# Second MLP, first layer: the first weight group as eight plain products instead of seven products of sums

## The chip, the cores and the metric

The kernel runs on one core of one Trainium2 chip. Times are device microseconds of one execution. The core's engines are TensorE (PE, with its weight loads PEld), VectorE (DVE), ScalarE (ACT), GpSimd (POOL) and SyncE (SP, which issues the DMAs). They run side by side and wait for one another by semaphores; each takes its own instructions in a fixed order.

## What is computed

Three stages follow one another: attention with a tanh cap on the scores, a gated MLP with RMS norm, and a second MLP. Only the last matters here.

```python
def _moe2_ref(x, w_in, w_out):          # x: 896 x 768, w_in: 768 x 2048
    h = x @ w_in
    g = h * (1.0 / (1.0 + np.exp(-h)))
    return (g @ w_out).astype(np.float32)
```

The change lies in the first 256 columns of `h = x @ w_in` and their silu.

## The kernel before, in words

Activations are kept transposed: features on the 128 partitions, 448 tokens (one of two batches) on the free axis. Products are made at nearly fp32 accuracy from two rounded halves of each operand: a high half (a rounded copy, mostly by ACT) and a low half (what the rounding left, a subtraction by DVE). A 128x128 block times 448 columns takes three matmuls: high times high, high times low, low times high; this text calls the three a triplet.

Every large matrix product is a 2x2 block product in Strassen-Winograd's form: seven block products of sums in place of eight plain ones. For the layer `h = x @ w_in`, `x` is cut into four operands, named by half of the features (K) and token batch: 11, 12, 21, 22. Each has three blocks of 128 features, `j` = 0 to 2. DVE turns them in place into T1 = 12 - 11, T3 = 22 - 12, T2 = 22 - T1 and T4 = 21 - T2 (`token_sums`, line 660), and each of 11, 21, 22, T1 to T4 is split into halves (`halves`: cast by ACT, low half by DVE on line 652).

The weights come in units of 128 hidden columns, two units `u`, `v` a group, eight groups i0 to i7. A unit is loaded by DMA and converted from its 8-byte form by two ACT operations (lines 349, 352) and one of DVE (line 355, tile `wz`). `sums` then makes four sums of `u` and `v` on DVE (lines 383, 386, 389, 392; tiles `zs`, `zq`), and `split` cuts `u`, `v` and the sums into halves (casts by ACT on line 287, low halves by DVE on line 370; tiles `wh`/`wl`, `sh`/`sl`, `qh`/`ql`).

`group` makes the seven products of a group, each of three triplets, on line 670: 11 and 21 with `u`, T2 with the sum, T1 with `v`, T3 with the sum, T4 with `v`, 22 with `zq`. They accumulate in PSUM banks of three rings, X (3 banks), Y (3) and Z (2). Partial results are read out between products by `keep` (ACT copies) and combined by three `add`s (DVE, line 773); silu follows on ACT (line 797).

The layer before it (the output layer of the gated MLP) writes the four operands from its own seven products, in the order 1, 2, 5, 6, 7, 3, 4. So 11 comes first (product 2), then 22 (product 7), then 12 (product 3, added from the Y banks on line 890), and 21 last (product 4, copied from the X banks by ACT).

The order of instructions is not that of the code. Each operation is entered with a list of engines and estimated costs, what it reads and writes, the buffers that it takes, and a priority from `turn` and a table by kind. A planner (`Plan.order`, eight rounds) lays out all operations after attention, sets each one's priority again from when its users are due, and keeps the best layout. GpSimd gets no work in this phase. A tile with one buffer of a name (`q5`, `p0`, ...) waits until all users of the one before are done.

Of the kernel before, what the change touches and what calls it, by code (L numbers as in the profile page):

```python
# [29 lines left out]
ROUNDS = 8  # L30
XS = 0.5
PE = 6
SWITCH = 0.1
WIN = dict(PE=0.05,ACT=0.50,DVE=0.50,Pool=0.25,SP=0.1,none=0.0)
BIAS1 = dict(ACT=0.0,DVE=0.0,Pool=0.0)
# [162 lines left out]
def fused_kernel(ctx: ExitStack, tc: tile.TileContext, qkv, cap, g, wg, wv, wo, wi2, wo2, out):  # L198
# [17 lines left out]
    S = NT // B  # L216
    P = 128
# [5 lines left out]
    KD = NP  # L223
# [4 lines left out]
    DH = DM // 2  # L228
# [4 lines left out]
    wp = ctx.enter_context(tc.tile_pool(name="wp", bufs=4))  # L233
# [3 lines left out]
    at = astack.enter_context(tc.tile_pool(name="at", bufs=2))  # L237
# [23 lines left out]
    op = plan.op  # L261
    tl = {}
# [11 lines left out]
    def half(name, n):  # L274
        return tl[name][:, n, :]
# [47 lines left out]
    def wide(name):  # L323

        t = tl[name]
        return t if len(t.shape) == 2 else f32(t.rearrange("p b s -> p (b s)"))[:, :UC]

    def convert(pl, u, turn, start=0.0, to="wz"):

        t = {}
        w, z, bufs = f"wraw_{u}", (f"wz_{u}.0", f"wz_{u}.1"), 1 if to[1:].isdigit() else 2

        def scale(e):
            words = wraw.pop(u)  # L340
            t["half"] = words.bitcast(U16).rearrange("p (n t) -> p n t", t=4)[:, :, 1]
            t["low"], high = (words.bitcast(U32).rearrange("p (n t) -> p n t", t=2)[:, :, i] for i in range(2))
            if bufs == 1:
                slot(f"wz_{u}", to)
            else:
                new(f"wz_{u}", wp, [P, UC], F32, to, bufs=2)
            z = wide(f"wz_{u}")
            t["zu"] = z.bitcast(U32)
            e.activation(out=z, in_=high.bitcast(F32), func=ACTF.Prelu, scale=2.0 ** -112, alpha=2.0 ** 32)  # L349

        def last(e):
            e.activation(out=t["low"], in_=t["half"], func=ACTF.Copy, scale=2.0 ** -13, bias=2.0 ** -14 - 0.5)  # L352

        def merge(e):
            e.scalar_tensor_tensor(t["zu"], t["zu"], 3, t["low"], ALU.logical_shift_left, ALU.bitwise_or)  # L355

        pl.op("wload", turn, lambda e: load_unit(u), {"SP": 0.45}, (), (w,), (("wraw", 2, w),), 0.66, 2.19, max(0.0, start - 6))
        pl.op("wscale", turn, scale, {"ACT": 0.81}, (w,), z, ((to, bufs, f"wz_{u}"),), start=start)
        pl.op("wshift", turn, last, {"ACT": 0.81}, z, (w,))
        pl.op("wlow", turn, merge, {"DVE": 0.87}, (w,), z)  # L360

    def split(pl, turn, z, reads, name, tags, pool, bufs=4, w=UC):

        h, l = f"h{name}", f"l{name}"

        def hi(e):
            copy(e, new(h, pool(), [P, w], F32R, tags[0], bufs=bufs), z())

        def lo(e):
            e.tensor_sub(new(l, pool(), [P, w], F32R, tags[1], bufs=bufs), z(), tl[h])  # L370

        full = w == UC
        pl.op("whi", turn, hi, {"ACT": 0.735, "DVE": 0.47} if full else {"ACT": 0.41, "DVE": 0.27}, reads, (h,), ((tags[0], bufs, h),))
        pl.op("wlo", turn, lo, {"Pool": 1.8, "DVE": 0.87} if full else {"Pool": 0.95, "DVE": 0.47}, (*reads, h), (l,), ((tags[1], bufs, l),))

    def sums(pl, u, v, turn, wait=()):

# [271 lines left out]
    def halves(pl, kinds, turn, name, tag, x):  # L649

        pl.op(kinds[0], turn, lambda e: copy(e, first(0, name, tag), x[1]()), {"ACT": 0.47, "DVE": 0.31}, (x[0],), (name + ".0",), ((tag, 1, name),))
        pl.op(kinds[1], turn, lambda e: e.tensor_sub(half(name, 1), x[1](), half(name, 0)), {"DVE": 0.54, "Pool": 1.1}, (x[0], name + ".0"), (name + ".1",))  # L652

    def token_sums(pl, kinds, turn, b, t, t2="22"):


        steps = (("11", "12", "11"), (t2, "22", "11"), ("12", "22", "12"), ("21", "21", t2))
        for i in (0, 2, 1, 3) if t2 == "22" else range(4):
            o, x, y = steps[i]
            pl.op(kinds[0], turn + 0.02 * max(0, i - 1), lambda e, o=o, x=x, y=y: e.tensor_sub(b[o][1](), b[x][1](), b[y][1]()), {"DVE": 0.54},  # L660
                  [b[m][0] for m in {x, y} - {o}], (b[o][0],), b[o][2] if len(b[o]) > 2 else ())
        for n, o in (("T2", t2), ("T1", "11"), ("T3", "12"), ("T4", "21")):
            halves(pl, kinds[1:], turn + 0.02 * "T2 T1 T3 T4".split().index(n), *t[n], b[o][:2])


    def passes(ps, w, c, x, start, stop, more=False):

        wh, wl = (tl[f"{n}{w}"][:, c:c + P] for n in "hl")
        for r, (a, y) in enumerate(((wh, x[0]), (wh, x[1]), (wl, x[0]))):
            nc.tensor.matmul(out=ps, lhsT=a, rhs=y, start=start and r == 0, stop=stop and r == 2, skip_group_check=more)  # L670
# [13 lines left out]
    for h in range(2):  # L684
        a, z = slice(h * R, (h + 1) * R), slice((1 - h) * R, (2 - h) * R)
# [19 lines left out]
    yo = ("11", "21", "T2", "T1", "T3", "T4", "22")  # L705
# [11 lines left out]
    order = plan.order(ROUNDS)  # L717
# [10 lines left out]
    class Rest(Plan):  # L728
        def op(self, kind, turn, fn, on, *args, **kw):

            super().op(kind, turn, fn, {e: c for e, c in on.items() if e != "Pool"}, *args, **kw)

    rest = Rest(TP2, DUE2, WIN2, BIAS2)
    op = rest.op

    def bank(name, tag):
        return new(name, mm, [P, 512], F32, tag, bufs=BANKS[tag])

    def take(name, tag):
        return (tag, BANKS.get(tag, 1), name)  # L740

    def group(n, u, v, turn, x, outs, stag):
# [44 lines left out]
        add(Y, 1, c12)  # L787
        return X

    def weights(u, v, turn):  # L790
        convert(rest, u, turn)
        convert(rest, v, turn)
        sums(rest, u, v, turn)

    def silu(turn, o, name, i=None, reads=(), alloc=()):
        src = i or o
        op("silu", turn, lambda e: e.activation(out=o(), in_=src(), func=ACTF.Silu), {"ACT": 0.5}, reads, (name,), alloc)
# [27 lines left out]
    def into(name, n, tag, on=True):  # L825

        def o():
            if on and name not in tl:
                slot(name, tag)
            return f32(half(name, n))  # L830
        return f"{name}.{n}", o
# [3 lines left out]
    for i in range(NG):  # L835
        h0, h1 = f"H_0_{i}", f"H_1_{i}"
        ta, tb, t0, t1 = ct[2 * i % 4], ct[(2 * i + 1) % 4], f"p{13 + i}" if i else "p20", f"q{12 + i}"
# [7 lines left out]
        X = group(f"g{i}", *g2, 2 * i, xop, outs, stags[0])  # L845
        for (name, o, _), t in ((outs[0], 0.3), (outs[3], 0.7), (outs[1], 0.9)):
            silu(2 * i + t, o, name)
        name, o = into(ca, 1, ta)
        silu(2 * i + 0.8, o, name, lambda X=X: tl[X][:, :S], (X,))
        houts = [(*into(h0, 0, t0), ((t0, 1, h0),)), (*into(h1, 0, t1), ()), None, (*into(h1, 1, t1), ((t1, 1, h1),))]  # L850
        X = group(f"v{i}", *v2, 2 * i + (1 if i else 0.05), xop, houts, stags[1])
        for n, c in ((0, f"{ca}.0"), (3, f"{cb}.1"), (1, f"{cb}.0")):
            name, o, _ = houts[n]
# [44 lines left out]
    t0, uo, MH, KH = 2 * NG, 2 * MF, MO // 2, MF // 2  # L898
# [11 lines left out]
    ty = dict(zip(yo, ("q12 q13 q14", "p16 p17 p18", "q9 q10 q11", "p9 p10 p11", "p20 p14 p15", "p0 p1 p2", "q15 q16 q17")))  # L910

    def ytag(y, j):
        return ty[y].split()[j]
# [4 lines left out]
    for i, n in enumerate(seq):  # L918
# [16 lines left out]
        for k in range(KH):  # L935
            h, c = hb(pb, k)
# [3 lines left out]
        for r in range(KH * MH):  # L940
            k, j = divmod(r, MH) if n != 4 else divmod(r, KH)[::-1]
            ps, w, x = f"{bank_of}_o{j}", f"o{n}_{j}", f"B{n}_{k}"

            def mul(e, k=k, ps=ps, w=w, x=x, fresh=fresh):
                if fresh and k == 0:
                    bank(ps, ps[0])
                passes(tl[ps][:, :S], w, k * P, (half(x, 0), half(x, 1)), fresh and k == 0, k == KH - 1, not fresh)

            op("mul", tn + 0.0476 * r, mul, {"PE": 0.595}, (f"h{w}", f"l{w}", *both(x)), (ps,), (take(ps, ps[0]),) if fresh and k == 0 else ())
        for j in range(MH):  # L950
            X, Y, Z, tj = f"X_o{j}", f"Y_o{j}", f"Z_o{j}", tn + 0.7
# [13 lines left out]
                evac("y", tj, X, yf(1, j, 1), y1 + ".1") if n == 4 else None  # L965
    for j in range(MH):
        ys = {y: (f"y{i}_{j}.{n}", yf(i, j, n)) for y, i, n in (("11", 0, 0), ("12", 0, 1), ("22", 1, 0), ("21", 1, 1))}
        for y in ("11", "22", "21"):
            halves(rest, ("tyh", "tyl"), t0 + 6, f"{y}_y{j}", ytag(y, j), ys[y])
        token_sums(rest, ("ty", "tyh", "tyl"), t0 + 6, ys, {n: (f"{n}_y{j}", ytag(n, j)) for n in yo[2:6]})  # L970


    ui, t0 = uo + 2 * MO, t0 + 6
    stile = "q5 q6 q7 q8 p3 p4 p5 q0 q1 q2 p12 p13 p19 p6 p7 p8".split()
    for i in range(MF2 // 2):
        u, v = ui + 2 * i, ui + 2 * i + 1
        weights(u, v, t0 + i)
        a, c = f"S_{2 * i}", f"S_{2 * i + 1}"
        qa, qc = stile[2 * i:2 * i + 2]
        outs = [(*into(a, 0, qa), ((qa, 1, a),)), (*into(a, 1, qa), ()), None, (*into(c, 1, qc), ((qc, 1, c),))]  # L980
        X = group(f"i{i}", u, v, t0 + i, lambda y, k: f"{y}_y{k}", outs, f"q{3 + i % 2}")
        for (name, o, _), t in ((outs[0], 0.3), (outs[3], 0.7), (outs[1], 0.9)):
            silu(t0 + i + t, o, name)
        name, o = into(c, 0, qc)
        silu(t0 + i + 0.8, o, name, lambda X=X: tl[X][:, :S], (X,))


    uw, t0 = ui + MF2, t0 + MF2 // 2
# [69 lines left out]
    for i, n in enumerate(seq):  # L1058
# [22 lines left out]
        for k in range(K2):  # L1081
            f, names, _ = sa(pa, k)
# [122 lines left out]
```

## Time and profile before

| | |
|---|---|
| median of 3 runs | 610.73 us (609.28 to 611.03) |
| the profiled execution | 611.11 us, span 609.0 us from first to last instruction |
| PE matmul busy | 591.4 us, 97% |
| PE weight loads busy | 498.8 us, 82% |
| DVE busy | 522.6 us, 86% |
| ACT busy | 456.0 us, 75% |
| mean granted TensorE clock | 0.988 of full speed |

Busy shares are averages over the whole span. A stretch with another limit than the rest has to be looked up in the sums by stretch, and what an engine waited for in its timeline and in the chain of waits.

### The profile page before, as it was taken

How to read it: one execution, taken by the hardware profiler on the slowest of the kernel's cores; microseconds unless marked ns; L12 is line 12 of the kernel's file. 1: busy time of each engine (PE TensorE's matmuls, PEld its weight loads, DVE VectorE, ACT ScalarE, POOL GpSimd, SP SyncE). 2: the span in 40 equal slices, each digit the busy share in tenths (PEclk: the TensorE clock that was granted, in tenths of full speed). 3: DMA queues.
4: the chain of work that ended last, by engine and by line, in shares of the span. 5: the costliest groups of instructions: out<-in, count | busy, mean ns of one | idle time of the engine just before them, and what ended most of it. 6: DMA issues, size and time to landing. Idle time of an engine off the chain costs nothing.

```text
span 609.0 us, 8752 instructions
## 1 busy us (share of the span) xinstructions
PE 591.4 (97%) x3170; PEld 498.8 (82%) x3170; DVE 522.6 (86%) x952; ACT 456.0 (75%) x807; POOL 52.6 (9%) x71
## 2 busy tenths in 40 slices
PE   7999999999899999999999999879999999999997
PEld 4555565557689999999999999669999999999997
DVE  4898999994998989868699999997878799999981
ACT  5998998882577776776796784866888889976642
POOL 1132429332000000000000000000000000000000
PEclk9999999999899999999999999969999999999999
DMA  6123212220025445343466001411534455440001
GB/s 259 52 106 97 111 54 73 92 97 0 2 103 163 150 142 169 104 156 107 153 206 208 2 0 50 159 53 52 180 132 156 156 166 195 159 155 1 34 31 66
DMA packets 15627, 66.23 MB, mean 109 GB/s; under 512 B 1888, under 2 KB 3680, under 8 KB 15584
## 3 DMA queue, kind: packets, MB, share of 16 engines
q1 hardware_dynamic: 15552, 65.67, 31.5%
q8 instruction: 25, 0.41, 0.3%
q14 instruction: 18, 0.15, 0.1%
q0 software_dynamic: 32, 0.00, 0.0%
HBM read 62.92 MB, written 2.75 MB: 108 GB/s over the span
## 4 chain that ended last, share of the span: by engine, by line
PE 64%; DVE 7%; ACT 2%; issue 1%; DMA 1%; DVEq 0%
PE X L670 29%; PE Y L670 15%; PE X L1037 7%; PE Z L670 7%; PE Y L1037 4%; DVE q L652 1%; PE Z L1037 1%; DVE p L660 1%; DVE p L355 1%; DMA wraw<-in_wo 1%; DVE wl L370 1%; ACT q L287 0%; DVE p L633 0%; DVE p L890 0%; DVE q L1090 0%
## 5 line engine op out<-in xcount | busy, mean ns | idle before, releaser
L670 PE MATMUL X<-q,sh 128*128 128x448 f32 x216 | 64.8, 379 | 6.0 <-DVE q L652 4.1
L352 ACT ACTIVATE wraw<-wraw 128x768 uint32<-128x768 uint16 x68 | 61.8, 908 | 0.0
L287 ACT COPY p<-X 128x448 f32<-128x448 f32 x48 | 25.6, 534 | 38.7 <-PE X L670 36.3
L670 PEld LDWEIGHTS X<-q,sh 128*128 128x128 f32 x216 | 42.0, 195 | 12.5 <-DVE q L652 5.7
L452 DVE TENSOR_SCALAR_CACHE_REDUCE p<-p,ncap 128x448 f32<-128x448 f32 x72 | 45.9, 674 | 6.9 <-ACT p L444 6.6
L670 PE MATMUL X<-q,wh 128*128 128x448 f32 x168 | 48.5, 368 | 1.5 <-DVE q L652 0.9
L370 DVE TENSOR_TENSOR wl<-wz,wh 128x768 fp32r<-128x768 f32 x47 | 44.8, 955 | 5.1 <-ACT wh L287 4.4
L287 ACT CAST wh<-wz 128x768 fp32r<-128x768 f32 x48 | 40.0, 836 | 11.0 <-DVE wz L386 4.7
L670 PE MATMUL X<-p,wh 128*128 128x448 f32 x168 | 48.1, 367 | 0.0
L355 DVE SCALAR_TENSOR_TENSOR wz<-wz,wraw 128x768 uint32<-128x768 uint32 x44 | 42.0, 956 | 5.2 <-ACT wraw L352 5.1
L287 DVE COPY pe<-pt 128x448 f32<-128x448 f32 x72 | 41.5, 618 | 5.6 <-PE pt L529 4.7
L287 ACT CAST q<-p 128x448 fp32r<-128x448 f32 (+1 forms) x51 | 27.3, 549 | 20.0 <-DVE p L931 6.0
L670 PE MATMUL X<-q,sl 128*128 128x448 f32 x108 | 40.6, 376 | 0.0
L349 ACT ACTIVATE wz<-wraw 128x768 f32<-128x768 f32 x44 | 39.9, 910 | 0.7 <-DVE wl L370 0.3
L444 ACT ACTIVATE p<-s,tscl 128x896 f32<-128x896 f32 x36 | 35.0, 1001 | 6.5 <-PE s L437 6.4
L670 PE MATMUL Z<-p,wh 128*128 128x448 f32 x132 | 38.9, 375 | 0.8 <-DVE p L652 0.8
L670 PEld LDWEIGHTS X<-q,wh 128*128 128x128 f32 x168 | 31.5, 188 | 5.3 <-DVE q L652 1.7
L437 PE MATMUL s<-x 64*128 64x448 f32 x144 | 33.2, 570 | 0.4 <-ACT p L444 0.3
L670 PEld LDWEIGHTS X<-p,wh 128*128 128x128 f32 x168 | 31.4, 188 | 2.6
L548 PE MATMUL av<-pe,x 128*64 128x448 f32 x144 | 31.7, 549 | 0.0
L287 ACT CAST p<-p 128x448 fp32r<-128x448 f32 (+1 forms) x47 | 25.3, 551 | 8.5 <-PE Y L1037 4.4
L670 PE MATMUL X<-q,wl 128*128 128x448 f32 x84 | 30.8, 367 | 0.3 <-DVE wl L370 0.3
(250 smaller groups left out, 1657.6 us busy)
## 6 DMA issues: line engine op xcount, KB each, us to landing
wraw<-in_wo SPq DMA_DIRECT2D x28, 768.0 KB, 4.3
wraw<-in_wi SPq DMA_DIRECT2D x16, 768.0 KB, 4.4
wraw<-in_wg SPq DMA_DIRECT2D x12, 768.0 KB, 4.6
wraw<-in_wv SPq DMA_DIRECT2D x12, 768.0 KB, 4.4
x<-in_qkv SPq DMA_DIRECT2D x11, 512.0 KB, 3.7
x<-in_qkv SPq DMA_DIRECT2D x14, 256.0 KB, 4.1
out<-q SPq DMA_DIRECT2D x12, 192.0 KB, 1.8
out<-zq SPq DMA_DIRECT2D x2, 192.0 KB, 1.9
```

The source lines that it names most:

```text
L287: e.tensor_copy(out=o, in_=i) if e is nc.vector else e.copy(out=o, in_=i)
L349: e.activation(out=z, in_=high.bitcast(F32), func=ACTF.Prelu, scale=2.0 ** -112, alpha=2.0 ** 32)
L352: e.activation(out=t["low"], in_=t["half"], func=ACTF.Copy, scale=2.0 ** -13, bias=2.0 ** -14 - 0.5)
L355: e.scalar_tensor_tensor(t["zu"], t["zu"], 3, t["low"], ALU.logical_shift_left, ALU.bitwise_or)
L370: e.tensor_sub(new(l, pool(), [P, w], F32R, tags[1], bufs=bufs), z(), tl[h])
L437: nc.tensor.matmul(out=ps[:, s, :S], lhsT=q_of(p, s, c), rhs=k_of(p, s), start=True, stop=True)
L444: nc.scalar.activation(out=o, in_=i, func=ACTF.Tanh, scale=tscl)
L452: nc.vector.tensor_scalar(t, t, ncap, None, ALU.mult, ALU.min, accum_out=tl[nb][:, n:n + 1])
L548: nc.tensor.matmul(out=tl[av][s * D:(s + 1) * D, :S], lhsT=v[:, (2 * k + s) * D:(2 * k + s + 1) * D], rhs=tl[f"pe_{p}_{m}"], start=k == 0, ...
L652: pl.op(kinds[1], turn, lambda e: e.tensor_sub(half(name, 1), x[1](), half(name, 0)), {"DVE": 0.54, "Pool": 1.1}, (x[0], name + ".0"), (na ...
L670: nc.tensor.matmul(out=ps, lhsT=a, rhs=y, start=start and r == 0, stop=stop and r == 2, skip_group_check=more)
L1037: nc.tensor.matmul(out=tl[ps][:, :DH], lhsT=y, rhs=x, start=start and r == 0, stop=stop and r == 2, skip_group_check=more)
```

## The change

For group i0 alone, `weights`, `group` and its silus are replaced. The two units are converted and split, with no sums (`operands`). `plain` makes eight products: each of the four results (12 and 22 for the second token batch, 11 and 21 for the first) is the sum of two products of plain weights and plain operands, accumulated in one PSUM bank of the rings Z and Y, and silu reads the bank. Products with operands 12 and 22 come first (four products), then those with 11 (two), then those with 21 (two). Operand 12, which had no halves, is now split as well; its halves take the slots (`p0 p1 p2`) that later hold those of T4. The halves of 12, 22, 11, 21 are entered with the turn that all had (`TYH` = 6.0), the token sums and the halves of T1 to T4 with a later one (`TY` = 6.2). Groups i1 to i7 stay as they are.

```diff
+TYH = 6.0
+TY = 6.2
...
+    def operands(pl, u, v, turn):
+        for x in (u, v):
+            split(pl, turn, lambda x=x: wide(f"wz_{x}"), (f"wz_{x}.0", f"wz_{x}.1"), f"w_{x}", ("wh", "wl"), lambda: wp)
...
+    def plain(n, u, v, turn, x, order, pauses=(0, 0, 0, 0)):
+
+        HK = KD // 2
+        left = {}
+        at = 0
+        for s, (c, tag, ys) in enumerate(order):
+            ps = f"{tag}_{n}{c}"
+            left[c] = left.get(c, 2)
+            for y in ys:
+                begin = left[c] == 2
+                left[c] -= 1
+                w, cols = f"w_{(u, v)[int(c[0]) - 1]}", DH * (int(y[0]) - 1)
+                for k in range(HK):
+                    def mul(e, k=k, y=y, ps=ps, w=w, cols=cols, begin=begin):
+                        if begin and k == 0:
+                            bank(ps, ps[0])
+                        passes(tl[ps][:, :S], w, cols + k * P, (half(x(y, k), 0), half(x(y, k), 1)), begin and k == 0, k == HK - 1, not begin)
+
+                    op("mul", turn + 0.14 * at + 0.04 * k + pauses[s], mul, {"PE": 0.595}, (f"h{w}", f"l{w}", x(y, k) + ".0", x(y, k) + ".1"), (ps,),
+                       (take(ps, ps[0]),) if begin and k == 0 else ())
+                at += 1
+        return {c: f"{tag}_{n}{c}" for c, tag, _ in order}
...
-        for y in ("11", "22", "21"):
-            halves(rest, ("tyh", "tyl"), t0 + 6, f"{y}_y{j}", ytag(y, j), ys[y])
-        token_sums(rest, ("ty", "tyh", "tyl"), t0 + 6, ys, {n: (f"{n}_y{j}", ytag(n, j)) for n in yo[2:6]})
+        for y in ("12", "22", "11", "21"):
+            halves(rest, ("tyh", "tyl"), t0 + TYH, f"{y}_y{j}", ytag("T4" if y == "12" else y, j), ys[y])
+        token_sums(rest, ("ty", "tyh", "tyl"), t0 + TY, ys, {n: (f"{n}_y{j}", ytag(n, j)) for n in yo[2:6]})
...
-        weights(u, v, t0 + i)
         a, c = f"S_{2 * i}", f"S_{2 * i + 1}"
         qa, qc = stile[2 * i:2 * i + 2]
+        if i == 0:
+
+            convert(rest, u, t0)
+            convert(rest, v, t0)
+            operands(rest, u, v, t0)
+            got = plain("i0", u, v, t0, lambda y, k: f"{y}_y{k}", (("12", "Z", ("12", "22")), ("22", "Y", ("12", "22")), ("11", "Z", ("11",)), ("21", "Y", ("11",)), ("11", "Z", ("21",)), ("21", "Y", ("21",))), (0,) * 6)
+            for n, (s, m, tag, t) in {"12": (a, 1, qa, 0.4), "22": (c, 1, qc, 0.7), "11": (a, 0, qa, 1.0), "21": (c, 0, qc, 1.1)}.items():
+                name, o = into(s, m, tag)
+                silu(t0 + t, o, name, lambda X=got[n]: tl[X][:, :S], (got[n],), ((tag, 1, s),) if n[1] == "2" else ())
+            continue
+        weights(u, v, t0 + i)
```

## Rows read from the trace of the kernel before

**Rows 1.** Busy time of each engine, share of the span, instructions.
```profile
PE 591.4 (97%) x3170; PEld 498.8 (82%) x3170; DVE 522.6 (86%) x952; ACT 456.0 (75%) x807; POOL 52.6 (9%) x71
```

**Rows 2.** Sums by stretch: window, length, busy time by engine, clock, DMA.
```profile
core 0: us, PE busy (x) PEld busy (x) DVE busy (x) ACT busy (x) POOL busy (x), PEclk, DMA share, GB/s
160.00:385.70 225.70, 225.41 (x1093) 205.99 (x1092) 201.03 (x307) 162.33 (x254) 0.00 (x0) 0.99 0.35 119
385.70:407.70 22.00, 16.18 (x55) 12.15 (x54) 21.97 (x38) 16.82 (x29) 0.00 (x0) 0.77 0.31 107
407.70:605.50 197.80, 197.69 (x1051) 189.21 (x1050) 167.38 (x270) 146.57 (x250) 0.00 (x0) 1.00 0.33 113
...
300.00:320.00 20.00, 20.00 (x100) 18.44 (x99) 19.63 (x30) 18.74 (x31) 0.00 (x0) 1.00 0.55 188
...
500.00:550.00 50.00, 49.92 (x284) 49.51 (x283) 48.17 (x80) 43.69 (x77) 0.00 (x0) 1.00 0.47 158
```

**Rows 3.** PE's timeline: start, us, instruction, count, idle before and releaser.
```profile
385.70 0.57 PE L670 MATMUL X<-q,wh 128*128 128x448 f32 x2
...
386.31 0.57 PE L670 MATMUL Z<-p,wh 128*128 128x448 f32 x2
...
398.23 0.74 PE L670 MATMUL X<-q,sh 128*128 128x448 f32 x1 [2.98 <-DVE q L652]
...
400.68 0.57 PE L670 MATMUL Z<-p,wh 128*128 128x448 f32 x1
...
407.71 0.57 PE L670 MATMUL Y<-p,wh 128*128 128x448 f32 x2
...
408.32 0.57 PE L670 MATMUL Y<-p,wh 128*128 128x448 f32 x2
```

**Rows 4.** Sums by stretch, microsecond by microsecond; the clock is third from the end.
```profile
397.00:398.00 1.00, 0.00 (x0) 0.00 (x0) 1.00 (x2) 0.64 (x1) 0.00 (x0) 0.50 0.00 0
...
406.00:407.00 1.00, 1.00 (x5) 0.90 (x4) 1.00 (x3) 0.45 (x1) 0.00 (x0) 0.65 1.05 418
407.00:408.00 1.00, 1.00 (x7) 0.93 (x6) 1.00 (x3) 0.17 (x2) 0.00 (x0) 1.00 0.60 238
```

**Rows 5.** Chain of waits from 376 to 420 us, two of its pieces.
```profile
384.63 0.07 DVE p L652
...
402.03 2.24 PE Z L670 x5
```

**Rows 6.** DVE's timeline.
```profile
376.31 0.96 DVE L355 SCALAR_TENSOR_TENSOR wz<-wz,wraw 128x768 uint32<-128x768 uint32 x1
377.18 1.17 DVE L652 TENSOR_TENSOR q<-p,q 128x448 fp32r<-128x448 f32 x2
...
380.53 0.55 DVE L383 TENSOR_TENSOR zs<-wz 128x384 f32<-128x384 f32 x1
...
381.60 0.62 DVE L652 TENSOR_TENSOR q<-p,q 128x448 fp32r<-128x448 f32 x1
...
386.24 0.96 DVE L355 SCALAR_TENSOR_TENSOR wz<-wz,wraw 128x768 uint32<-128x768 uint32 x1
...
405.57 0.95 DVE L370 TENSOR_TENSOR wl<-wz,wh 128x768 fp32r<-128x768 f32 x1
406.44 2.76 DVE L652 TENSOR_TENSOR p<-p,p 128x448 fp32r<-128x448 f32 x5
409.12 0.62 DVE L660 TENSOR_TENSOR p<-p 128x448 f32<-128x448 f32 x1
...
415.48 0.55 DVE L370 TENSOR_TENSOR ql<-zq,qh 128x384 fp32r<-128x384 f32 x1
415.94 0.62 DVE L773 TENSOR_TENSOR q<-q,Z 128x448 f32<-128x448 f32 x1
```

**Rows 7.** ACT's timeline.
```profile
391.09 2.14 ACT L287 CAST p<-p 128x448 fp32r<-128x448 f32 x4
```

**Rows 8.** PE's timeline: the last triplet of the layer before into a Y bank.
```profile
374.68 0.57 PE L670 MATMUL Y<-p,sh 128*128 128x448 f32 x2
```

## The prediction, made before the change was run

> **What bounds the kernel now.** The shares of the whole span come first: TensorE (PE) is 97% busy, so at first sight nine more matmuls cost what they last [rows 1]. The sums by stretch say where that fails. From 160 us to the start of the changed group and from its recovery to the last matmul, PE is busy without a hole. In the 22.0 us between, it is busy for 16.2 us at a mean granted clock of 0.77, while VectorE (DVE) has 21.97 of 22.00 [rows 2]. That is the only place where PE loses time, and it is the start of the changed group.
>
> How much it loses is read from PE's timeline. The first matmul of group i0 starts at 385.70 us, and full rate is back from 407.71 [rows 3]. A triplet (one K block in three passes) takes 0.61 us at full clock (385.70 to 386.31, and again 407.71 to 408.32). In that stretch PE did 18 triplets (54 matmuls; the window counts 55, as it takes in the end of the one before): 18 x 0.61 = 11.0 us of work in 22.0, so 11.0 us are lost. Its longest wait, 2.98 us, ends with a low half written by DVE [rows 3]. After the waits the granted clock is at its lower level, 1.2 GHz (0.50 of full), from before 397 until within 406 to 407 us, then full again [rows 4].
>
> The chain of waits names the cause: it leaves PE for DVE at 384.63 and comes back to PE at 402.03 [rows 5]; the pieces between, nearly all DVE's, are sums and low halves. DVE's list sets the stretch. DVE is nearly full long before (19.63 of 20 us at 300), so work can't be moved ahead to there [rows 2].
>
> **The change part by part.** Prices are from start to next start on DVE's timeline, as its instructions overlap a little [rows 6]: a 448-column operation 0.536 us (five from 406.44 to 409.12 = 2.68), a 768-column one 0.87 (376.31 to 377.18; 405.57 to 406.44), a 384-column weight sum 0.53 (two from 380.53 to 381.60 = 1.07), the low half of the 384-column sum 0.46 (415.48 to 415.94).
>
> *Removed on DVE:* four weight sums 2.13, low half of zs 0.87, of zq 0.46, three adds of kept partial results 1.61; together 5.07. *Added:* low halves of operand 12, three, 1.61. Net 3.46 us less. *ScalarE (ACT):* two weight casts and three keeps go and three casts of 12 come, each about 0.5 us (four casts take 2.14 [rows 7]); silu reads PSUM instead of SBUF, same count. ACT has 16.82 of 22 us in the stretch, so this costs nothing while that reserve of 5 us lasts; without it, half a microsecond for each cast. *PE:* eight products instead of seven, 9 matmuls or 3 triplets more: 3 x 0.61 = **+1.83 us**. After the stretch PE runs full to the end, so they are paid in full. *Queues:* no DMA is added or removed; only SP issues in this phase, one per weight unit as before.
>
> *Moved:* the token sums and the halves of T1 to T4. Group i0 no longer waits for them; group i1, a whole group later, does. That is the larger effect, and I work it out as DVE's list in the order that PE needs it, from 376.31 us, against PE at full rate from 385.70 (a product is 1.83).
>
> - Operands 12 and 22 with both weights: one last low half for the layer before (0.54), four 768-column operations (3.48), three adds that finish 12, one add that frees a Z bank, six low halves (10 x 0.536 = 5.36): ready at 385.7. 12's last product ends at about 375.3 [rows 8], so nothing earlier holds it, and these operands carry four products, to 393.0.
> - 11 and 21: one add and six low halves, 3.75: ready at 389.4, needed from 393.0 (21 itself from 396.7). Group i0 can run through to 385.70 + 8 x 1.83 = 400.3.
> - Group i1: first weight 1.74, ready 391.2, needed 400.3. T2: second weight's conversion 0.87, three weight sums 1.60, low half 0.87, nine token sums 4.82, three low halves 1.61: ready 400.9, needed 404.0. T1 (2.48) 403.4, needed 405.8. T3 (1.61) 405.0, needed 407.7. T4 (3.22) 408.3, needed 409.5.
> - Then s4 and its low half (0.99), i1's three adds (1.61), i2's first weight (1.74) and its sums (3.34): ready 415.9, needed 416.8.
>
> The list is never late; its smallest reserves are about 1 us. The same list for the kernel before gives T4 of i0 ready at 401.6 (25.25 us of work) where PE wants it at 394.9, a stall of 6.7. The trace has 11.0: 4.3 us more than the list, since DVE converts i1's weights in between (386.24 [rows 6]) and the clock falls. So the loss left after the change lies between 0 (the list) and 4.3 - 0.9 = 3.4 (the same excess on the new list). I take 1.5, nearer the low end, because i1's weights, which caused much of the excess, are now in the list.
>
> *New waits.* T4's halves take the slots that held 12's. Product 4 is the last to read those, at about 393; T4's casts come after 405, so neither they nor what stands behind them on ACT waits. The weight halves of i2 need the slots of i0's first weight, which the plain form reads until its seventh product, about 398.5; before, that weight's last product started at 400.68 [rows 3]. No wait is added there. If 12 came late instead, PE would idle from 385.7 with all of i0 behind it.
>
> **The sum**, against the profiled execution's own 611.11 (span 609.0): 611.11 - 11.0 + 1.5 + 1.83 = 603.4. The median of the runs shown is 0.38 lower, 610.73, so the prediction is **603.0 us**. What can be told from no change is 0.3%, 1.8 us.
>
> Over the span DVE is 86% busy, PE's weight loads 82% and its matmuls 97% [rows 1]. The Trainium skill, in "Perfetto Trace Analysis", section "Identifying the Most-Contended Engine", counts TensorE by weight loads and not by matmul time, and says to work on the engine with the highest share. By that DVE binds the kernel as a whole, and a change is worth what it takes off DVE. The rows by stretch bear it out in the 22 us only; the time that it would give is the second rival's.
>
> **The rivals.**
> 1. *The stall moves into group i1.* The list's reserves there are 1 to 3 us, and DVE, ACT and PE take their work in a fixed order. One handover of 2.98 us, as in [rows 3], takes up the reserve at T4, and the clock falls again as in [rows 4]. For: the list has 39.6 us of work for the 40.5 us from 376.3 to 416.8. Against: i1 also has 22 and T3, and i2's first product, to put between. A loss of 3.4 to 6.5: 604.9 to 608.0.
> 2. *Only what leaves DVE's list counts.* If the token sums still stand ahead of the halves of 12 and 11, all of it is before i0's end as now: 610.73 - 3.46 + 1.83 = 609.1. Against: the sums overwrite 11, 12 and 22 in place, so those halves must be cut first.
> 3. *Slower.* DVE converts i1's weights, splits one and makes and splits the sums (1.74 + 0.87 + 2.13 + 0.87 = 5.6 us) before 12's halves, as at 386.24 it does before i0's operands are done. PE then idles at i0's start, its clock halves, and the 11.0 stay, with 1.83 more: 612.6. It decides as soon as more than 9.2 of the 11.0 remain. Against: 12 is complete 10 us before it is needed.
> 4. *The change does not do only this.* One planner orders all work after attention, and new operations can shift that order elsewhere. At 300 to 320 DVE has 0.37 us spare and at 500 to 550 1.83 [rows 2]; each microsecond lost there adds one. 2 to 6 us: 605 to 609.
>
> **How the numbers follow.** Forecast (loss 0 to 3.4: 601.5 to 604.9) 0.58; rival 1 0.17; rival 2 0.08; rival 3 0.10; rival 4 0.07. Range: below, no loss at all, 601.5, less 0.3 for the spread of the runs, 601.2; above, rival 1's end, 608.0. It holds the forecast, rival 1 and most of rival 4: 0.58 + 0.17 + 0.05 = 0.80. Faster by over 0.3% (under 608.9): 0.58 + 0.17 + 0.03 of rival 2 + 0.05 of rival 4 = 0.83; slower: rival 3, 0.10; the rest, 0.07, within.
>
> **What would show it.** Right: PE's matmuls on Z and Y with the new halves start near 385.7 and run as triplets of 0.61 us for some 14.6 us; the mean granted clock from 385 to 408 is near 1.00; DVE is still full until about 413; the chain of waits stays on PE. The span from the last triplet of i1 to the end is as before. Wrong: a hole in PE at i1's T2 to T4 with a low half as the releaser (rival 1); the same hole at i0 (2 or 3); holes after 420 or before 385 (4).

## The result, and the profile after

The changed kernel takes 601.03 us (median of 4 runs, 599.66 to 602.29), the kernel before on the same chip 610.15 (4 runs): a ratio of 0.9846, 95% interval 0.9825 to 0.9867. That is 9.1 us less, where 7.7 were forecast from 610.73 to 603.0. The direction and the place were right; the time lies 0.17 us under the range's lower end, 601.2.

The shares of the whole span say little, as before [rows 1]: PE has 9 matmuls more and is busy for 4.2 us less. Most of that lies in the 22 us of [rows 2], where 55 matmuls had been busy for 16.18 us; at full rate (0.61 / 3 = 0.204 us each) they are 11.2.

```profile
PE 587.2 (98%) x3179; PEld 498.5 (83%) x3179; DVE 518.4 (87%) x946; ACT 454.7 (76%) x805; POOL 52.7 (9%) x71
```

The sums by stretch show where it went. The first line below covers the 22 us from the start of group i0 and answers to the line of [rows 2] with 16.18 us of PE and a clock of 0.77. The others are stretches of 10 us around it; the columns are those of [rows 2].

```profile
384.80:406.80 22.00, 22.00 (x110) 20.29 (x109) 21.15 (x38) 16.87 (x31) 0.00 (x0) 1.00 0.28 86
...
385.00:395.00 10.00, 10.00 (x51) 9.23 (x50) 10.00 (x19) 5.57 (x11) 0.00 (x0) 1.00 0.49 159
395.00:405.00 10.00, 10.00 (x51) 9.23 (x50) 9.15 (x16) 9.30 (x17) 0.00 (x0) 1.00 0.00 0
405.00:415.00 10.00, 10.00 (x51) 9.15 (x50) 9.93 (x19) 6.94 (x14) 0.00 (x0) 1.00 0.38 130
415.00:425.00 10.00, 9.82 (x49) 8.72 (x48) 9.49 (x15) 9.62 (x16) 0.00 (x0) 1.00 0.54 185
```

PE is busy for all 22.00 us, with 110 matmuls instead of 55, at full clock; DVE is nearly as full as before (21.15 us, where it had 21.97). PE's timeline agrees: i0 starts at 384.78, i1's T2 follows at 403.09 without a wait, and the one hole left is 0.17 us at 420.00, ended by an ACT copy.

```profile
384.78 0.56 PE L676 MATMUL Z<-p,wh 128*128 128x448 f32 x2
...
403.09 0.57 PE L676 MATMUL X<-q,sh 128*128 128x448 f32 x2
...
419.05 0.57 PE L676 MATMUL Y<-p,wh 128*128 128x448 f32 x2
...
420.00 0.67 PE L676 MATMUL X<-p,sh 128*128 128x448 f32 x2 [0.17 <-ACT q L289]
```

From the first matmul of i0 to the end of the span it was 609.0 - 385.7 = 223.3 us before [rows 3] and is 598.9 - 384.8 = 214.1 now: 9.2 less. That is 11.0 - 1.83, the sum with no loss at all. (The span is shorter by 10.1; the other 0.9 us lie ahead of the change.)

### The profile page after: what moved, and what is told of

Read it like the earlier page. It is cut to its first block, busy times and chain, and to the rows that moved or that the text cites. A ratio compares the mean times of both kernels' runs of the same rounds, so it can differ in the third digit from the quotient of the medians.

```text
span 598.9 us, 8749 instructions
## 1 busy us (share of the span) xinstructions
PE 587.2 (98%) x3179; PEld 498.5 (83%) x3179; DVE 518.4 (87%) x946; ACT 454.7 (76%) x805; POOL 52.7 (9%) x71
## 4 chain that ended last, share of the span: by engine, by line
PE 66%; DVE 5%; ACT 1%; issue 1%; DVEq 0%; ACTq 0%
PE X L676 28%; PE Y L676 16%; PE X L1076 8%; PE Z L676 8%; PE Y L1076 5%; PE Z L1076 2%; DVE wl L372 1%; DVE p L658 1%; DVE p L666 0%; DVE p L357 0%; DVE p L639 0%; DVE q L1129 0%; DVE q L658 0%; DVE zs L907 0%; ACT wz L351 0%
## 5 line engine op out<-in xcount | busy, mean ns | idle before, releaser
L676 PE MATMUL X<-q,sh 128*128 128x448 f32 x210 | 60.7, 369 | 2.7 <-ACT q L289 1.6
L676 PE MATMUL X<-q,wh 128*128 128x448 f32 x162 | 46.4, 367 | 0.1
L676 PE MATMUL X<-p,wh 128*128 128x448 f32 x162 | 46.4, 368 | 0.0
L676 PEld LDWEIGHTS X<-q,sh 128*128 128x128 f32 x210 | 39.6, 189 | 7.6 <-ACT q L289 2.0
L676 PE MATMUL X<-q,sl 128*128 128x448 f32 x105 | 38.6, 368 | 0.0
L289 ACT CAST p<-p 128x448 fp32r<-128x448 f32 (+1 forms) x50 | 27.0, 552 | 12.4 <-DVE p L666 5.0
L676 PEld LDWEIGHTS X<-p,wh 128*128 128x128 f32 x162 | 30.2, 188 | 2.5
L676 PE MATMUL Y<-q,wh 128*128 128x448 f32 x108 | 31.8, 375 | 0.2 <-DVE q L658 0.2
```

The costliest lines, as they stand in the source:

```text
L289: e.tensor_copy(out=o, in_=i) if e is nc.vector else e.copy(out=o, in_=i)
```

## The experiments

For each run stand the median, that of the kernel before in the same session, and the ratio with its 95% interval. Where a line of the sums by stretch is shown, it is that of 380 to 430 us, which holds the whole stretch in every kernel. A trace is of one execution. A matmul takes 0.204 us at full rate, so the 50 us hold 245; each one missing from that is 0.204 us lost. The kernel before:

```profile
380.00:430.00 50.00, 44.18 (x192) 37.88 (x191) 45.47 (x77) 35.47 (x60) 0.00 (x0) 0.90 0.31 102
```

and the changed one:

```profile
380.00:430.00 50.00, 49.83 (x245) 45.58 (x244) 46.89 (x78) 40.65 (x68) 0.00 (x0) 1.00 0.36 124
```

So the kernel before loses 53 x 0.204 = 10.8 us, as the prediction counted (11.0) by triplets.

**1. The changed kernel once more.** No edit.

> The changed kernel once more, on the same chip as the next three. The measured -9.1 us against the kernel before is what the list of VectorE's work gives when no loss is left at all (-11.0 + 1.83 = -9.2). If that is so, it comes out at 0.985 of the kernel before again, 600 to 602 us. If the first measurement was a lucky draw and 1.5 us of loss are left in most runs, it comes out at 602.5 to 603.5, 0.987 to 0.989.

Measured: 601.16 us beside 609.86, ratio 0.9861 (0.9839 to 0.9883). The theory's number. Its trace too has 245 matmuls in the 50 us.

**2. Seven products without the weight sums.** An edit of the kernel before; the sums' places are taken by the first unit's plain halves.

```diff
+        if n == "i0":
+            steps = tuple((ps, f"w_{w[2:]}" if w[0] in "sq" else w, c, y, z) for ps, w, c, y, z in steps)
...
-        weights(u, v, t0 + i)
+        if i:
+            weights(u, v, t0 + i)
+        else:
+            for x in (u, v):
+                convert(rest, x, t0)
+            for x in (u, v):
+                split(rest, t0, lambda x=x: wide(f"wz_{x}"), (f"wz_{x}.0", f"wz_{x}.1"), f"w_{x}", ("wh", "wl"), lambda: wp)
```

> The kernel before with seven products in group i0, but without i0's weight sums: where the sums of the two weight units stood, the first unit's plain halves are used, so the first 256 columns are not the reference's. It takes four 384-column sums, their two low halves (3.46 us of VectorE) and two casts off the list and leaves everything else, the wait for T1 to T4 above all. Theory (VectorE's list sets the stall, and the token sums are its larger part): of the list's work ahead of T4, 2.5 us go, and VectorE is still late by about 4.2 us where it was 6.7; the time falls by 2.5 to 4.6 us with the slow clock's share, to 605.5 to 607.7. Rival (what leaves VectorE's list is all that counts, and the order does nothing): it falls by as much as the changed kernel without its price, 9 to 11 us, to 599 to 601.

Measured: 604.86 us beside 609.86, ratio 0.9913 (0.9897 to 0.9930).

```profile
380.00:430.00 50.00, 47.04 (x216) 40.91 (x215) 45.48 (x74) 39.04 (x65) 0.00 (x0) 0.97 0.32 111
```

The loss is 29 x 0.204 = 5.9 us where it was 10.8. The shorter list alone, with the wait for T1 to T4 as it was, gives 5.0 us, slightly more than forecast and about half of the 10.9 that the change recovers (9.1 and its price of 1.83). It isn't all that counts.

**3. Eight products with the weight sums kept.** An edit of the changed kernel; the four sums and their halves are made and not used.

```diff
+    def unused_sums(u, v, turn):
+        a, b, c, d = f"wz_{u}", f"wz_{v}", f"zs_{u}", f"zq_{u}"
...
+        rest.op("sum", turn, s3, on, (a + ".0", b + ".0"), (c + ".1",), (("zs", 2, c),))
+        rest.op("sum", turn, lambda e: e.tensor_add(tl[c][:, h[0]], tl[b][:, h[0]], tl[b][:, h[1]]), on, (b + ".0", b + ".1", c + ".1"), (c + ".0",))
+        rest.op("sum", turn, lambda e: e.tensor_sub(tl[c][:, h[0]], tl[c][:, h[0]], tl[a][:, h[0]]), on, (a + ".0",), (c + ".0",))
+        rest.op("sum", turn, s4, on, (a + ".1", c + ".0"), (d,), (("zq", 2, d),))
+        split(rest, turn, lambda: tl[c], (c + ".0", c + ".1"), f"s_{u}", ("sh", "sl"), lambda: wp, 2)
+        split(rest, turn, lambda: tl[d], (d,), f"q_{u}", ("qh", "ql"), lambda: wp, 2, DH)
...
+            unused_sums(u, v, t0)
```

> The changed kernel, but group i0's four weight sums and the halves of the two sum tiles are still made, as before, and used by nothing: the eight plain products and the later token sums without the shorter list (3.46 us of VectorE and two ScalarE casts more; the output stays the reference's). They have to be begun before group i1's own, since they take turns in the same buffers. Theory by the prediction's list, whose smallest reserve is 0.9 us: a loss of 3.46 - 0.9 = 2.6 us, to 603.6. Rival (the list is too strict, since TensorE has other groups' products with 11 and 21 to put between): no loss, 600 to 602. If the shorter list were what counts, most of the gain would go: over 607.

Measured: 604.62 us beside 609.86, ratio 0.9909 (0.9891 to 0.9927).

```profile
380.00:430.00 50.00, 48.01 (x230) 41.94 (x229) 48.38 (x81) 38.94 (x65) 0.00 (x0) 1.00 0.34 112
```

The later token sums alone are worth 5.2 us, the price of 1.83 included, or 7.1 without it. Against experiment 1 it is 3.5 us slower by the medians (1.2 to 4.6 by the two intervals taken together), and it loses 15 x 0.204 = 3.1 us by the count, for 3.46 us of DVE. So the runs can't tell the list's 2.6, with its reserve of 0.9, from 3.46 without one. No loss at all, the rival, is out.

**4. The four operands' low halves twice.** An edit of the changed kernel.

```diff
+            rest.op("tyl", t0 + TYH, lambda e, n=f"{y}_y{j}", x=ys[y]: e.tensor_sub(half(n, 1), x[1](), half(n, 0)), {"DVE": 0.54}, (ys[y][0], f"{y}_y{j}.0"), (f"{y}_y{j}.1",))
```

> The changed kernel, but the low halves of 12, 22, 11 and 21 are each made twice over (the same result; 12 more 448-column operations, 12 x 0.536 = 6.4 us of VectorE, at the place where group i0's own operands are made). Theory by the prediction's list: 6.4 - 0.9 = 5.5 us of loss, to 606.6, and a hole in TensorE with VectorE as the releaser. Rival (products of later groups fill in): under half of that, 601 to 603.8.

Measured: 608.09 us beside 609.86, ratio 0.9969 (0.9956 to 0.9983): 6.9 us over experiment 1 by the medians (5.0 to 8.2 by the two intervals) for 6.4 us of DVE, where the list with its reserve gave 5.5. The sums by stretch, then PE's timeline:

```profile
380.00:430.00 50.00, 45.97 (x213) 39.95 (x212) 49.48 (x83) 34.26 (x58) 0.00 (x0) 0.97 0.31 108
...
405.00:410.00 5.00, 2.29 (x7) 1.22 (x7) 5.00 (x9) 5.00 (x11) 0.00 (x0) 0.95 0.00 0
410.00:415.00 5.00, 4.77 (x18) 4.12 (x18) 5.00 (x10) 3.81 (x6) 0.00 (x0) 0.71 0.19 60
```

```profile
405.21 0.47 PE L676 MATMUL X<-q,sh 128*128 128x448 f32 x1 [0.44 <-ACT q L289]
407.53 0.48 PE L676 MATMUL X<-q,sh 128*128 128x448 f32 x1 [1.84 <-DVE q L658]
```

The loss is 32 x 0.204 = 6.5 us, and the lower clock (0.71 from 410 to 415 us) is part of it. The hole sits where i1's T2 product begins, a group later than in the kernel before, and DVE ends it: this is what the prediction's first rival describes. Experiments 3 and 4 together put the changed kernel near the point where DVE's list begins to cost: it has no loss and little reserve.

**5. Two groups by eight plain products.** An edit of the changed kernel.

```diff
-        if i == 0:
+        if i < 2:
...
+            got = plain(f"i{i}", u, v, t0 + i, ...
...
```

> The changed kernel with group i1 by eight plain products as well (T1 to T4 are wanted one group later still, VectorE's list loses another 3.46 us, TensorE gets 9 more matmuls). Theory: with 0.4 us of loss left after the change there is nothing more to win, and the second extra product is paid in full: 1.83 - 0.4 = 1.4 us over the changed kernel, 602.3 to 602.8. Rival (plain products with fewer sums are cheaper in themselves, since VectorE is the fuller engine by weight loads): it gains again, by up to 3 us, to 598 to 600.

Measured: 601.67 us beside 610.29, ratio 0.9861 (0.9844 to 0.9878). The ratio is that of experiment 1, so the runs can't tell the price of 1.4 us from none; they exclude a gain of 3 us.

```profile
380.00:430.00 50.00, 50.00 (x247) 46.11 (x246) 45.10 (x73) 38.78 (x66) 0.00 (x0) 1.00 0.36 128
```

PE has no hole left, and DVE is down to 45.10 us of 50. By the profiled executions, from the first product of the gated MLP (145.49 us in experiment 1, 145.11 here) to the end of the span (599.0 and 600.2) it is 453.5 and 455.1: 1.6 us more, near the price.

```profile
145.49 0.65 PE L676 MATMUL X<-p,wh 128*128 128x448 f32 x2
```

```profile
145.11 0.65 PE L676 MATMUL X<-p,wh 128*128 128x448 f32 x2
```

**6. The last operand first.** An edit of the changed kernel.

```diff
-            got = plain("i0", u, v, t0, lambda y, k: f"{y}_y{k}", (("12", "Z", ("12", "22")), ("22", "Y", ("12", "22")), ("11", "Z", ("11",)), ("21", "Y", ("11",)), ("11", "Z", ("21",)), ("21", "Y", ("21",))), (0,) * 6)
...
+            got = plain("i0", u, v, t0, lambda y, k: f"{y}_y{k}", (("11", "Z", ("21",)), ("21", "Y", ("21",)), ("11", "Z", ("11",)), ("21", "Y", ("11",)), ("12", "Z", ("12", "22")), ("22", "Y", ("12", "22"))), (0,) * 6)
...
```

> The changed kernel with the order of the eight products turned round: those with operand 21 first, then 11, then 12 and 22. 21 is written by the last product of the layer before, copied by ScalarE, cast and subtracted; in the changed kernel its low halves end at 389.7, 390.2 and 391.6 us, where TensorE is free from 384.8. Theory: with 21 due first, TensorE has only its first block early, and loses about what 21's last block is late, less what other products fill in: 2 to 5 us, to 603 to 606. Rival (the order does nothing, since the planner takes whatever product is ready): within 0.3% of the changed kernel.

Measured: 601.24 us beside 610.29, ratio 0.9857 (0.9838 to 0.9876). The theory fell. ACT's timeline shows the three copies that make operand 21; first in the changed kernel, then here:

```profile
380.10 0.53 ACT L289 COPY p<-X 128x448 f32<-128x448 f32 x1 [0.93 <-PE X L676]
...
386.33 0.53 ACT L289 COPY p<-X 128x448 f32<-128x448 f32 x1
...
388.02 0.56 ACT L289 COPY p<-X 128x448 f32<-128x448 f32 x1
```

```profile
379.25 0.53 ACT L289 COPY p<-X 128x448 f32<-128x448 f32 x1 [0.86 <-PE X L676]
...
382.81 0.55 ACT L289 COPY p<-X 128x448 f32<-128x448 f32 x1
...
385.52 0.51 ACT L289 COPY p<-X 128x448 f32<-128x448 f32 x1
```

The planner brought 21 forward, by up to 3.5 us, and mixes the products on PE by what is ready. The order in which the products are entered is a wish, and the gain does not hang on it.

**7. Group i1's weights held back, seven products.** An edit of the kernel before: VectorE's merge (`wlow`) of i1's weights also reads T3's low halves.

```diff
-        pl.op("wlow", turn, merge, {"DVE": 0.87}, (w,), z)
+        pl.op("wlow", turn, merge, {"DVE": 0.87}, (w, *wait), z)
...
-        weights(u, v, t0 + i)
+        weights(u, v, t0 + i, tuple(f"T3_y{j}.1" for j in range(MH)) if i == 1 else ())
```

> The kernel before (seven products in group i0), with one more condition: VectorE's merge of group i1's two weights waits until the low halves of T3 are made, so that VectorE does all of i0's own work first, as the list in the prediction has it. That list gave a loss of 6.7 us where the trace has 11.0; the prediction laid the other 4.3 to i1's weights done in between and to the slow clock. Theory: the loss falls to about 6.7 to 8, 605.5 to 607.5. Rival (the planner's mixture was the best use of VectorE, and the work kept back is missed later): no better than before, 609 to 613.

Measured: 609.86 us beside 610.29, ratio 0.9992 (0.9977 to 1.0007). The theory fell.

```profile
380.00:430.00 50.00, 44.41 (x196) 37.68 (x195) 43.34 (x72) 34.55 (x58) 0.00 (x0) 0.93 0.28 95
```

The loss is 49 x 0.204 = 10.0 us. The merges held back, DVE is busy 2.1 us less in this stretch than in the kernel before, and PE is no further. PE's timeline shows why. From 385.79 us PE does all of i0 but T4 in a row, 18 triplets, with holes of up to 1.46 us, and then i1's first product waits for its weights. The kernel before starts that product at 388.21, inside i0's holes. First this run, then the kernel before:

```profile
391.54 0.48 PE L670 MATMUL X<-q,sh 128*128 128x448 f32 x1 [1.46 <-DVE q L652]
...
406.66 0.68 PE L670 MATMUL X<-q,wh 128*128 128x448 f32 x2 [0.25 <-ACT wh L287]
```

```profile
388.21 0.68 PE L670 MATMUL X<-q,wh 128*128 128x448 f32 x2 [0.52 <-ACT wh L287]
```

So i1's weights done in between cost i0 about what they bring to i1.

**8. The first gate group plain too.** An edit of the changed kernel, in the gated MLP, which starts after attention.

```diff
-        sums(plan, u, v, 2 * i + 2)
+        operands(plan, u, v, 2 * i + 2) if i == 0 else sums(plan, u, v, 2 * i + 2)
...
+        halves(rest, ("txh", "txl"), 0.01 * k, f"G12_{k}", tplace("T4", k), xs["12"])
...
+        if i == 0:
+            got = plain("g0", *g2, 0, lambda y, k: f"G12_{k}" if y == "12" else xop(y, k), (("11", "Z", ("11", "21")), ("21", "Y", ("11", "21")), ("12", "Z", ("12", "22")), ("22", "Y", ("12", "22"))), (0,) * 4)
...
```

> The changed kernel, with the same edit at the only other place where TensorE waits after attention: the first gate group of the gated MLP (holes of 0.54, 1.59, 0.60 and 0.20 us at 155 to 160 us, 2.9 in all, each ended by a low half of VectorE's). Eight plain products, those with 11 and 21, which are ready from attention, first; 12 is split as well, in the slots of T4. Theory: a hole is worth closing so only as far as it is longer than the product added: -2.9 + 1.83 = 1.1 us less than the changed kernel, near 600. Rival (this stretch has more VectorE work with 12's halves and the hole stays or moves into the second group): the price alone, 1.8 us more, 603.

Measured: 602.17 us beside 610.29, ratio 0.9868 (0.9851 to 0.9885): no gain over experiment 1. The holes at 155 to 160 us were gone, but the first product of the gated MLP started late:

```profile
150.55 0.65 PE L676 MATMUL Z<-p,wh 128*128 128x448 f32 x2
```

That is 5.1 us later than in experiment 1. The weight sums of this group are made during attention, and taking them out had changed attention's order; experiment 9 tests that. One reading in the text above is wrong: the longest of the four holes ends with a cast of ACT's, not with a low half, as the changed kernel's timeline has it:

```profile
157.70 0.47 PE L676 MATMUL X<-q,sh 128*128 128x448 f32 x1 [1.59 <-ACT q L289]
```

**9. The same with attention's order kept.** As experiment 8, but the sums stay, written beside the second unit.

```diff
+            e.tensor_add(tl[c if whole else b][:, h[0]], tl[b][:, h[0]], tl[b][:, h[1]])
...
+            e.tensor_sub(tl[c][:, h[0]], tl[c if whole else b][:, h[0]], tl[a][:, h[0]])
...
+        sums(plan, u, v, 2 * i + 2, whole=i == 0)
```

> The changed kernel with the first gate group plain as well, as in the run before this one, but with the weight sums of that group still made during attention (used by nothing, and written beside the second weight unit instead of over it), so that the order of the work in attention stays what it was. In the run before, TensorE's holes at 155 to 160 us were gone, and from the first product of the gated MLP to the end it took 450.6 us where the changed kernel takes 453.5; but attention ended 5 us later, since its order had been planned anew without the sums. Theory: without that, the 2.9 us are seen: 598 to 599, 0.980 to 0.982 of the kernel before. Rival (attention ended later because the plain group's operands were wanted then, not because its order was planned anew): 601 to 603 again.

Measured: 597.91 us (597.35 to 598.04) beside 610.50, ratio 0.9795 (0.9771 to 0.9818). It beats both kernels; the time lies just under the theory's, and the rival's 601 to 603 is out. From 145 to 165 us, in experiment 1 and then here:

```profile
145.00:165.00 20.00, 17.09 (x84) 14.64 (x84) 14.39 (x27) 9.81 (x17) 1.03 (x1) 0.91 0.00 1
```

```profile
145.00:165.00 20.00, 20.00 (x108) 18.63 (x109) 15.16 (x29) 12.90 (x23) 1.03 (x1) 1.00 0.00 1
```

PE is full where it had waited 2.9 us and run slowly after. 24 matmuls more in the 20 us are 4.9 us; less 1.83 for the added product that leaves 3.1, and the span is 595.6 where experiment 1 has 599.0.

**10. One turn for both.** An edit of the changed kernel.

```diff
-TY = 6.2
+TY = 6.0
```

> The changed kernel with the token sums entered at the same turn as the operands' halves (6.0 in place of 6.2). Theory: the planner sets every priority again from when its users are due, so the turn decides nothing in the end: within 0.3% of the changed kernel, 600 to 602.5. Rival (the later turn is what keeps the token sums out of the way of group i0's operands): most of the gain goes, 605 to 610.

Measured: 601.35 us beside 610.50, ratio 0.9853 (0.9829 to 0.9877). The two turns do nothing that the runs can tell. In this run's trace, too, the first token sum starts after the last low half of i0's operands (392.80 us), as in the changed kernel (392.03, after 391.03):

```profile
393.81 0.62 DVE L666 TENSOR_TENSOR p<-p 128x448 f32<-128x448 f32 x1
```

**11. The longest hole filled, seven products.** An edit of the kernel before.

```diff
+FILL = 14
...
-                    if start and k == 0:
+                    if start and k == 0 and ps != "Y_i0":
                         bank(ps, ps[0])
+                    if y == "T2" and k == 0 and ps == "X_i0":
+                        bank("Y_i0", "Y")
+                        for _ in range(FILL):
+                            nc.tensor.matmul(out=tl["Y_i0"][:, :S], lhsT=tl[f"hw_{u}"][:, :P], rhs=half(x("11", 0), 0), start=True, stop=True)
```

> The kernel before, with 14 unused matmuls (14 x 0.204 = 2.9 us at full clock) put ahead of group i0's first T2 matmul, in the longest hole (394.98 to 398.23 us); they write a PSUM bank that the T1 product begins anew, and nothing in the order of the work changes. It asks what of the loss of 11.0 us is the fallen clock and not the wait itself. Theory: the clock stays at its upper level. The three triplets from 402.95 to 406.31 us, which wait for nothing, took 3.36 us at the lower level, 1.83 at the upper; the next product's low half is ready at 405.66: 1.5 to 2 us less, 608.2 to 608.7. Rival 1 (the slow matmuls are hidden behind VectorE): no change, 610.2. Rival 2 (the clock holds all that the list doesn't explain): 4.3 us less, 606.

Measured: 608.85 us beside 610.50, ratio 0.9972 (0.9955 to 0.9989), 1.65 us less (0.7 to 2.7 by the interval): the theory's number, and both rivals out. By the trace, i0's start to T1's first matmul takes 19.9 us (385.08 to 404.98) where it took 22.0 (385.70 to 407.71 [rows 3]), 2.1 less.

PE's timeline has the 14 unused matmuls and, after them, triplets of 0.61 us each, where the kernel before took 1.12 (3.36 / 3). First this run, then the kernel before:

```profile
393.71 3.01 PE L763 MATMUL Y<-q,wh 128*128 128x448 f32 x14
...
402.54 0.57 PE L671 MATMUL X<-q,sh 128*128 128x448 f32 x2
...
403.15 0.57 PE L671 MATMUL X<-q,sh 128*128 128x448 f32 x2
```

```profile
402.95 0.95 PE L670 MATMUL Z<-p,wh 128*128 128x448 f32 x2
...
406.31 0.76 PE L670 MATMUL X<-q,sh 128*128 128x448 f32 x2
```

The sums by stretch give a granted clock of 1.00 just after them, where the kernel before has 0.50, the lower level:

```profile
398.00:399.00 1.00, 0.48 (x3) 0.10 (x1) 1.00 (x3) 0.88 (x2) 0.00 (x0) 1.00 0.00 0
```

```profile
398.00:399.00 1.00, 0.77 (x2) 0.73 (x3) 1.00 (x3) 0.26 (x1) 0.00 (x0) 0.50 0.00 0
```

## Why the prediction missed its range

*What bounds the kernel: right for the stretch.* The change recovered the whole of the one stretch, and nothing outside it. That it is the only place where PE loses time goes too far: PE also waits 2.9 us between 155 and 160 us, ahead of the rows that the prediction read, and experiment 9 wins that back.

*The loss left after the change: this step failed, by its size.* The prediction put it between 0 (DVE's list) and 3.4 (the list with the excess of the kernel before) and took 1.5. It is 0 by the count of matmuls, and the one hole costs under 0.4 us. The allowance was borrowed from the 4.3 us by which the kernel before lost more than its list, and its trace shows that the list did not describe that loss. By the list PE waits for T4 of i0, ready at 401.6 us. In the trace the longest hole and the last one end with low halves of T2 (398.23 us [rows 3]) and of 21 (402.03). By their banks and tiles the 18 triplets of the stretch are those of 11, 21 and T2, nine of i0 and nine of i1, and T4 begins at 413.88, when full rate has been back for 6 us:

```profile
402.03 0.74 PE L670 MATMUL Z<-p,wh 128*128 128x448 f32 x1 [0.78 <-DVE p L652]
...
413.88 0.57 PE L670 MATMUL X<-p,wh 128*128 128x448 f32 x2
```

So neither the 6.7 us of the list nor the 4.3 beyond it is a part of that loss that could be carried over. Experiment 11 shows about 1.65 us of the loss to be the fallen clock, which a kernel without a hole does not pay, and by experiment 7 i1's weights done in between cost about what they bring. How the rest of the 11.0 us divides stays open.

For the changed kernel the list said no loss, which is what came, but the order that ran was not the list's. It has T4 of i1 ready at 408.3; the last of T4's token sums starts at 412.04 and its last triplet at 415.37. PE has no hole there, since it puts i2's products with 11 (from 408.63) and 21 ahead, as the prediction's case against its first rival said. So it is in part luck that the list's answer held. The lines are PE's, then DVE's, then PE's:

```profile
408.63 0.57 PE L676 MATMUL X<-q,wh 128*128 128x448 f32 x2
...
412.04 0.62 DVE L666 TENSOR_TENSOR p<-p 128x448 f32<-128x448 f32 x1
...
415.37 0.57 PE L676 MATMUL X<-p,wh 128*128 128x448 f32 x2
```

*The lower end: too high.* It was the sum without loss, less 0.3, from a median of three runs, 610.73. In the sets of runs taken with the result and since, the kernel before has medians of 610.15, 609.86, 610.29 and 610.50. The sum without loss from those is 600.7 to 601.3, and the changed kernel's medians are 601.03 and 601.16. A case that is the best possible and also likely needs more room below it than the spread of three runs.

*The reserves of about 1 us: not seen, and not excluded.* By the count of matmuls experiments 3 and 4 lose 3.1 and 6.5 us, where the list with its reserve gave 2.6 and 5.5; but the timed runs hold both, and in experiment 4 the fallen clock is part of the loss. The chain of waits of the changed kernel speaks for little reserve. The prediction expected it to stay on PE; it leaves PE at 401.4 us and returns at 420.0, through ACT's weight conversion and DVE:

```profile
400.80 0.62 PE X L676 x3
...
401.87 0.91 ACT wz L351
...
404.48 2.23 DVE p L658 x4
...
420.00 5.14 PE X L676 x24
```

DVE's timeline has a wait there that the list has not, 0.85 us for ACT:

```profile
403.60 0.96 DVE L357 SCALAR_TENSOR_TENSOR wz<-wz,wraw 128x768 uint32<-128x768 uint32 x1 [0.85 <-ACT wraw L354]
```

It is about as long as the smallest reserve in the list. That it used the reserve up is argued, not shown.

*What moves and what is saved: right in kind.* Alone, the later token sums give 7.1 us (5.2 and the price), the shorter list 5.0; together 10.9 of 11.0. They overlap, since the second finds only what the first left.

*The price of 1.83 us: consistent, not resolved.* The changed kernel's sum closes with it, and experiment 5's trace has 1.6 us for the next one; its timed runs can't tell it from nothing.

*The rivals.* The first did not come. Experiment 4's 6.4 us of DVE bring it, with the fallen clock; experiment 3's 3.5 us bring short holes at full clock. The second fell with experiments 2 and 3. The third had its condition wrong: the halves of 12 were made in time. Of the fourth there is no trace after 435 us or before 380. It came instead in experiment 8, in attention, and cost 5.1 us.

The section "Identifying the Most-Contended Engine" of "Perfetto Trace Analysis" in the Trainium skill goes by the highest share of the span, with TensorE counted by its weight loads, and so would put DVE first. Relieving DVE without moving its deadline (experiment 2) gave about half of what the change recovers; the measurement decides for reading it by stretch.

## What to carry to other kernels

Where one engine fills a short stretch and the engine behind it waits, write the waiting engine's needs as a list in order with measured prices, and ask which can come a group later; a product more on the waiting engine is cheap as long as the hole is longer than it. Before carrying over what the old kernel lost beyond its list, look in the trace whether its holes lie where the list puts them; here the list had T4 and the trace T2 and 21. Test a reserve by doubling an operation before relying on it. When an order is planned by program, taking out operations can replan work far ahead of them: keep them as unused work to see the edit's own worth (experiments 8 and 9 differ by over 4 us).

## What the hardware showed beyond that

The granted clock fell without a long single wait. In experiment 4 the longest wait was 1.84 us, with 0.44 before it and more holes after it (PE busy 2.29 of 5 us), and the mean clock of the next 5 us was 0.71. In experiment 3 waits of 0.2 to 0.5 us, scattered over 20 us, left it at 1.00. In experiment 2 it fell after a longest wait of 1.39 us (0.71 from 395 to 400 us); in experiment 11, whose longest wait in this stretch is 1.39 us as well, it stayed at 1.00 there. Experiment 2, then experiment 11:

```profile
393.58 0.47 PE L670 MATMUL X<-q,wh 128*128 128x448 f32 x1 [1.39 <-DVE q L652]
...
395.00:400.00 5.00, 4.92 (x17) 4.03 (x17) 4.96 (x10) 1.70 (x3) 0.00 (x0) 0.71 0.00 0
```

```profile
401.41 0.48 PE L671 MATMUL Z<-p,wh 128*128 128x448 f32 x1 [1.39 <-DVE p L653]
```
